# Keys, queries and values in token order: a change to how windowed attention gets its key tiles

## The chip, the cores and the metric

The kernel runs on one NeuronCore of a Trainium2 chip. The metric is the device time of one execution, in microseconds (us). A core has five engines, each with its own queue of instructions that it works off in order: PE (TensorE, the matrix unit; its weight loads are listed as PEld), DVE (VectorE), ACT (ScalarE), POOL (GpSimd) and SP (SyncE). DMA transfers are issued by SP and POOL here and run on 16 DMA engines beside them. A transfer that changes the type (a cast from float32 to bfloat16) is issued by POOL, a transfer that transposes by SP.

## What is computed

Attention over a window with eight global tokens, for 8 batches x 8 heads x 576 tokens x 64 dimensions, and then a two-layer network on the joined heads (4608 tokens, 512 -> 2048 -> 512), whose activation is h + sin(alpha h)^2 / alpha:

```python
scores = scale * np.matmul(q, k.transpose(0, 1, 3, 2))
mask = np.abs(pos[:, None] - pos[None, :]) <= 32
mask = mask | is_global[:, None] | is_global[None, :]
attn = softmax(np.where(mask, scores, -1e9))
x = (attn @ v).transpose(0, 2, 1, 3).reshape(B * S, H * D)
h = x @ w_in
s = np.sin(alpha * h)
out = (h + s * s / (alpha + 1e-09)) @ w_out
```

## The kernel before

**Stages.** The work is done batch by batch. `attention(b)` makes scores, weights, sums and the normalised x of batch b, transposed (`xT`). `gemm1(b)` multiplies by `w_in` in 16 groups of 128 columns (`nt`): PE makes a group of 8 matmuls in one of three PSUM tiles (`zn`, `zr`, `zd`), ACT takes the sine (L1192), ACT or DVE squares it (L1195, L1197), DVE adds and writes `H2` (L1198) and so frees the tile. `gemm2(b)` multiplies by `w_out`; its matmuls (L1250) are a generator, from which `fill` puts some between the other stages' matmuls on PE. The program is `phase_a(0)`, `gemm1(0)`, `phase_a(1)`, `gemm1(1)` and so on, where `phase_a(b)` is attention(b) with gemm2(b-1) mixed in. The instructions of an engine stand in the order of the program text.

**Key tiles.** The 576 keys of a batch are cut into 12 tiles of 48. A tile takes 64 columns of `KX`: its keys, the 8 global keys (`NG`), and zeros. Two heads lie on the 128 partitions. The rows of `VX` or `VF` (values) and of the mask have the same order as the columns of `KX`. Before, that order is: 24 even tokens, 8 global, 24 odd tokens, 8 empty. There are two `KX`, `QX` (queries, even and odd tokens apart) and value buffers, for even and odd batches.

**How batches 2 to 7 get their keys and queries.** `cast_qk(b)` (L334) casts keys and queries into DRAM (`kd`, `qd`) in large pieces, as they lie. `turn_qk(b)` (L350) transposes each in one DMA on SP into `kt` and `qt`. `place(b, which, t, y)` (L358) copies them on DVE into `KX` (L370) and `QX` (L363), in eight copies of 64 partitions x 1152 a batch: `which` is key or query, `t` the half of the tokens, `y` even or odd. `PLACES` lists the eight; `places_at` and the two tables `PLACED_SECOND` and `PLACED_LATE` say where they are done: for batch 2, two at the end of attention(1) and six in gemm1(1); for later batches, the four of keys in the attention stage before, at the third and fourth pair of heads, and the four of queries in the gemm1 that follows, at groups 5, 7, 9 and 11.

**Batches 0 and 1** get keys and queries another way (`load_lying`, `turn_lying`, `place_lying`: loaded with a cast by POOL, transposed on PE, copied from PSUM).

**Values.** For batches 2 to 7, `cast_v(b)` (L344) casts into DRAM by tokens and heads (`vd`, 4608 pieces of 64 elements), `load_v(b)` (L433) loads them in four DMAs and `load_vg(b)` (L437) adds the global rows. Batch 0 is loaded with a cast by POOL in twelve DMAs (`load_v0`, L396), tokens in pairs; DVE copies the odd rows to their place (`odd_rows`, L415) and four edge tiles are copied to `VE` (`edge_tile`, L419). Batch 1 is cast in pairs to `vpd` (L402), loaded in two DMAs (L408), and treated by `odd_rows` and `edge_tile` in the same way. In these two batches the global values are multiplied apart (`global_products`, L927, with weights `VGT`).

**What sets the order of the DMAs.** POOL issues casts and loads in one queue; `pace` (L348) is a small copy of some result, behind which POOL's next casts wait. SP issues transposes, loads, the stores of the output (L1283, from three tiles `osb`) and a store of logarithms for each pair of heads (L823, from five tiles). A DMA of either queue waits until the one eight before it has landed.

Of the kernel before, what the change touches and what calls it, by code (L numbers as in the profile page):

```python
# [29 lines left out]
PLACES = [(w, t, y) for w in (1, 0) for t in range(2) for y in range(2)]  # L30
# [220 lines left out]
def kernel(  # L251
# [47 lines left out]
    VF = [main.tile([P, NT6, H, 2, D], DT.bfloat16, name=f"VF{i}") for i in range(2)]  # L299
    VE = [main.tile([P, H, D], DT.bfloat16, name=f"VE{i}") for i in range(2)]  # L300
    vflat = [t[:].rearrange("p m h y d -> p (m h y d)") for t in VF]
# [12 lines left out]
    VGT = [main.tile([P, H, D], DT.bfloat16, name=f"VGT{i}") for i in range(2)]  # L314
    gkq = [main.tile([NG * B, NG, D], DT.bfloat16, name=f"gkq{i}") for i in range(2)]
    pick = main.tile([NG * B, 2, P], DT.bfloat16, name="pick")
# [14 lines left out]
    vpd = dramp.tile([HALF, H, 2, D], DT.bfloat16, name="vpd")  # L331

    def cast_qk(b):

        for src, name in ((k, "kd"), (q, "qd")):
            cast[b, name] = dramp.tile([P, H * S * D // P], DT.bfloat16, name=name)
            flat = (cast[b, name][:].rearrange("p f -> (p f)"), src[b].rearrange("h s d -> (h s d)"))
            dst, src_b = [t.rearrange("(a e c) -> e a c", a=16, e=16) for t in flat]
            nc.gpsimd.dma_start(out=dst, in_=src_b)

    def cast_v(b):

        cast[b, "vd"] = dramp.tile([S, H, D], DT.bfloat16, name="vd")
        nc.gpsimd.dma_start(out=cast[b, "vd"][:], in_=v[b].rearrange("h s d -> s h d"))  # L344
# [5 lines left out]
    def turn_qk(b):  # L350

        turned[b] = [trp.tile([P, H * HALF], DT.bfloat16, name=name) for name in ("qt", "kt")]
        for i in (1, 0):
            nc.sync.dma_start_transpose(
                out=turned[b][i][:], in_=cast[b, ("qd", "kd")[i]][:].rearrange("p (r c) -> (p r) c", c=P)
            )

    def place(b, which, t, y, copy, hps=slice(0, NHP)):  # L358

        src = turned[b][which][:].rearrange("p (hp t s) -> p t hp s", t=2, s=HALF)[y * D : (y + 1) * D, t, hps]  # L360
        rows = slice(t * D, (t + 1) * D)
        if which == 0:
            copy(  # L363
                out=QX[b % 2][rows, hps, y, PAD : PAD + 6 * SEG].rearrange("p h (m c) -> p h m c", c=SEG)[
                    :, :, :, 4:
                ],
                in_=src.rearrange("p h (m a) -> p h m a", a=KT),
            )
        else:
            copy(  # L370
                out=KX[b % 2][rows, hps, :, y * 32 : y * 32 + NH],
                in_=src.rearrange("p h (i a) -> p h i a", a=NH),
            )

    def place_globals(b, part, copy):

        if part == 0:
            copy(out=KX[b % 2][:, :, :, NH : NH + NG], in_=kTg[:, :, None, :, b].to_broadcast([P, NHP, NT12, NG]))
# [14 lines left out]
    def load_v0():  # L393
        for half in range(2):
            for m in range(NT6):
                nc.gpsimd.dma_start(  # L396
                    out=VF[0][half * D : half * D + NH, m].rearrange("p h y d -> p h (y d)"),
                    in_=v[0].rearrange("h (n m a y) d -> n m a h (y d)", n=2, a=NH, y=2)[half, m],
                )

    def cast_v1():
        nc.gpsimd.dma_start(  # L402
            out=vpd[:].rearrange("s h y d -> s h (y d)"), in_=v[1].rearrange("h (s y) d -> s h (y d)", y=2)
        )

    def load_v1():
        for half in range(2):
            nc.sync.dma_start(  # L408
                out=VF[1][half * D : half * D + NH].rearrange("p m h y d -> p m (h y d)"),
                in_=vpd[:].rearrange("(n m a) h y d -> n a m (h y d)", n=2, a=NH)[half],  # L410
            )

    def odd_rows(b, half, copy):
        r = half * D
        copy(out=VF[b][r + 32 : r + 32 + NH, :, :, 0], in_=VF[b][r : r + NH, :, :, 1])  # L415

    def edge_tile(b, half, y, copy):
        r, m, o = (1 - half) * D, half * (NT6 - 1), half * D + y * 32
        copy(out=VE[b][o : o + NH], in_=VF[b][r : r + NH, m, :, y])  # L419

    def edge_tiles(b, half, copy):
        for y in range(2):
            edge_tile(b, half, y, copy)

    def load_v(b):


        for half in range(2):
            m0 = half * (NT6 - 1)
            src = cast[b, "vd"][:].rearrange("(m a y) h d -> y a m (h d)", a=NH, y=2)[:, :, m0 : m0 + NT6 + 1]  # L430
            for y in range(2):
                r = half * D + y * 32
                nc.sync.dma_start(out=VX[b % 2][r : r + NH].rearrange("p m h d -> p m (h d)"), in_=src[y])  # L433

    def load_vg(b):
        for r in (NH, D + NH):
# [5 lines left out]
    def values(b, rows, half, i, h):  # L442

        if b > 1:
            return VX[b % 2][rows, i - half * (NT6 - 1), h, :]
        m = i - half * NT6
        return VF[b][rows, m, h, 0, :] if 0 <= m < NT6 else VE[b][rows, h, :]

# [58 lines left out]
    nc.gpsimd.iota(place8[:], pattern=[[0, 2], [NG, D]], base=-NG * NH, channel_multiplier=0,  # L507
# [18 lines left out]
    for t in (0, D):  # L526
        nc.sync.dma_start(out=gp64[t + NH : t + NH + NG], in_=global_idx[:, None])
        nc.sync.dma_start(
            out=gidx8[t + NH : t + NH + NG],
# [31 lines left out]
    for i, bits in enumerate((B - 1, D - 1, B * (NG - 1))):  # L561
# [6 lines left out]
    cond = setup.tile([P, 4], DT.float32, name="cond")  # L568
    odd, isg, off, iskey = [cond[:, i : i + 1] for i in range(4)]
    nc.vector.tensor_scalar(out=odd, in0=pm, scalar1=32.0, scalar2=None, op0=ALU.is_ge)  # L570
    nc.vector.scalar_tensor_tensor(out=isg, in0=pm, scalar=float(NH), in1=odd, op0=ALU.is_ge, op1=ALU.subtract)
    nc.vector.scalar_tensor_tensor(out=off, in0=pm, scalar=float(NK), in1=isg, op0=ALU.is_ge, op1=ALU.add)
    nc.vector.tensor_scalar(out=iskey, in0=off, scalar1=-1.0, scalar2=1.0, op0=ALU.mult, op1=ALU.add)
    nc.vector.tensor_scalar(out=kpos[:], in0=pm, scalar1=2.0, scalar2=None, op0=ALU.mult)
    nc.vector.scalar_tensor_tensor(out=kpos[:], in0=odd, scalar=-63.0, in1=kpos[:], op0=ALU.mult, op1=ALU.add)
    nc.vector.scalar_tensor_tensor(
        out=kpos[:], in0=off, scalar=float(4095 + KT), in1=kpos[:], op0=ALU.mult, op1=ALU.add
    )
# [864 lines left out]
```

## Time and profile before

| | us |
|---|---|
| median of 3 runs (lowest to highest) | 343.82 (343.78 to 345.46) |
| the profiled execution | 346.34 |
| its span, first to last instruction | 344.6 |
| mean granted PE clock | 0.995 |

The columns of the view of stages (windows) are: the stretch and its length, then busy time and count of instructions of PE, PEld, DVE, ACT and POOL, the granted clock of PE, the busy share of the DMA engines (over 1 where packets overlap) and the GB/s that they moved. A row of a group of instructions gives the line, engine and operation, the tiles written and read with their shape, the count, the busy time in us and the mean of one in ns, and the idle time before them. A row of the timeline gives start and duration in us; "[x <-y]" behind it is idle time ahead of it and what ended it. A row of the chain gives start, duration and what was done then on the path that ended last. SPq and POOL rows of DMAs are the time that it took to issue them.

### The profile page before, as it was taken

Reading aid. Unit: us, or ns where it says so; the run is one execution under the profiler, and the core shown is the slowest. Engines: PE = TensorE matmul, PEld = TensorE weight load, DVE = VectorE, ACT = ScalarE, POOL = GpSimd, SP = SyncE. Lnnn points to the kernel's source line nnn. Section 1 sums busy time; section 2 is a strip of 40 time slices with the busy share of each in tenths; the row PEclk is TensorE's granted clock in tenths of the full one; section 3 lists DMA queues with packets and bytes.
Section 4 is the critical chain, followed back from the end, with each engine's and each line's share of the span. In section 5 each row is a group of like instructions: output and inputs, shape, how many; then the busy total and the mean of one; then the engine's idle time right before and its main releaser. Section 6 shows DMA issues by size and latency. Waiting matters only on the chain.

```text
span 344.6 us, 11604 instructions
## 1 busy us (share of the span) xinstructions
PE 313.9 (91%) x4791; PEld 202.3 (59%) x4851; DVE 274.4 (80%) x535; ACT 282.8 (82%) x410; POOL 57.1 (17%) x90
## 2 busy tenths in 40 slices
PE   0778999999997999999999999999999999999993
PEld 0646765666554764677556655676566655665553
DVE  5886899789985698879886889789787988788930
ACT  9886988888997679988899789978898888889611
POOL 7982120120240000400040002200000000003600
PEclk9999999999998999999999999999999999999999
DMA  7999999999999546798449942993624111010232
GB/s 103 117 168 202 199 221 175 167 169 188 172 149 194 120 47 155 133 208 127 102 83 221 162 84 56 199 163 73 129 74 86 30 32 66 3 31 2 77 93 68
DMA packets 83021, 41.79 MB, mean 121 GB/s; under 512 B 65442, under 2 KB 74002, under 8 KB 82962
## 3 DMA queue, kind: packets, MB, share of 16 engines
q0 software_dynamic: 41600, 18.50, 43.3%
q1 hardware_dynamic: 41362, 22.48, 30.1%
q8 instruction: 39, 0.64, 0.8%
q14 instruction: 20, 0.16, 0.1%
HBM read 41.85 MB, written 20.77 MB: 182 GB/s over the span
## 4 chain that ended last, share of the span: by engine, by line
PE 66%; DMA 11%; DVE 7%; issue 5%; ACT 4%; POOL 4%; DVEq 0%; POOLq 0%; ACTq 0%
PE zo L1250 31%; PE zn L1150 10%; DMA w_out<-in_moe_w_out_dram 8%; PE zd L1150 7%; PE zr L1150 7%; DVE H L1198 5%; DMA w_in<-in_moe_w_in_dram 3%; PE ring L863 3%; PE zd L911 2%; PE zn L911 2%; POOL VF L396 2%; ACT sb L1192 2%; DVE s L1197 1%; DVE QX L363 1%; ACT s L1195 1%
## 5 line engine op out<-in xcount | busy, mean ns | idle before, releaser
L1250 PE MATMUL zo<-w_out,H 128*128 128x512 bf16 (+1 forms) x516 | 135.1, 378 | 6.3 <-issue 5.1
L1150 PEld LDWEIGHTS <-w_in 128*128 128x128 bf16 x1024 | 99.8, 98 | 50.0 <-issue 16.4
L1250 PEld LDWEIGHTS <-H 128*128 128x128 bf16 x592 | 54.0, 98 | 47.1 <-issue 1.3
L1150 PE MATMUL zn<-xT,w_in 128*128 128x288 bf16 (+1 forms) x384 | 57.0, 287 | 3.5 <-DVE H L1198 2.9
L1150 PE MATMUL zr<-xT,w_in 128*128 128x288 bf16 x320 | 47.9, 287 | 2.6 <-issue 2.0
L1192 ACT ACTIVATE sb<-zn,alphaT 128x576 bf16<-128x576 f32 (+1 forms) x48 | 35.6, 742 | 15.9 <-PE zn L1150 15.5
L1198 DVE SCALAR_TENSOR_TENSOR H<-s,recipT,zn 128x576 bf16<-128x576 bf16 (+1 forms) x48 | 39.5, 822 | 10.5 <-ACT s L1195 6.4
L1150 PE MATMUL zd<-xT,w_in 128*128 128x288 bf16 x320 | 47.1, 291 | 0.5 <-DVE H L1198 0.2
L871 ACT ACTIVATE E<-ring 128x720 bf16<-128x720 f32 x46 | 36.0, 782 | 9.4 <-PE ring L863 8.8
L1197 DVE TENSOR_TENSOR s<-sb 128x576 bf16<-128x576 bf16 (+1 forms) x70 | 32.6, 466 | 12.4 <-ACT sb L1192 12.1
L1195 ACT ACTIVATE s<-sb 128x576 bf16<-128x576 bf16 (+1 forms) x58 | 40.0, 689 | 1.8
L880 DVE TENSOR_TENSOR E<-E,MASKT 128x720 bf16<-128x720 bf16 x64 | 33.3, 528 | 5.6 <-ACT E L871 3.7
L1198 DVE SCALAR_TENSOR_TENSOR H<-s,recipT,zd 128x576 bf16<-128x576 bf16 (+1 forms) x40 | 32.9, 822 | 3.8 <-ACT s L1195 1.1
L1198 DVE SCALAR_TENSOR_TENSOR H<-s,recipT,zr 128x576 bf16<-128x576 bf16 (+1 forms) x40 | 32.9, 822 | 3.1 <-ACT s L1195 0.7
L1192 ACT ACTIVATE sb<-zd,alphaT 128x576 bf16<-128x576 f32 (+1 forms) x40 | 29.6, 739 | 5.9 <-PE zd L1150 5.9
L1192 ACT ACTIVATE sb<-zr,alphaT 128x576 bf16<-128x576 f32 (+1 forms) x40 | 29.6, 739 | 5.3 <-PE zr L1150 5.2
L1257 ACT COPY osb<-zo 128x512 f32<-128x512 f32 (+1 forms) x36 | 21.0, 583 | 10.7 <-PE zo L1250 7.0
L863 PEld LDWEIGHTS <-KX 64*64 64x64 bf16 x896 | 15.7, 113 | 19.6 <-issue 19.0
L828 ACT ACTIVATE R<-L,shift 128x576 f32<-128x576 f32 x32 | 25.0, 785 | 1.3 <-DVE xT L954 0.8
L1240 POOL COPY H<-H 128x11 bf16 (+1 forms) x16 | 7.2, 453 | 99.0 <-DVE H L1198 98.1
L348 POOL COPY seen<-xT 1x1 bf16<-1x1 bf16 x4 | 1.9, 479 | 106.7 <-DVE GN L805 106.7
L954 DVE TENSOR_TENSOR xT<-zn,R 128x576 bf16<-128x576 f32 x22 | 16.6, 753 | 2.9 <-ACT R L828 0.9
(181 smaller groups left out, 361.9 us busy)
## 6 DMA issues: line engine op xcount, KB each, us to landing
VF<-vd SPq DMA_DIRECT2D x24, 168.0 KB
kd<-in_k_dram POOLq DMA_DIRECT2D x6, 576.0 KB, 8.3
qd<-in_q_dram POOLq DMA_DIRECT2D x6, 576.0 KB, 16.1
vd<-in_v_dram POOLq DMA_DIRECT2D x6, 576.0 KB, 13.0
w_in<-in_moe_w_in_dram POOLq DMA_DIRECT2D x2, 1024.0 KB, 15.9
w_out<-in_moe_w_out_dram POOLq DMA_DIRECT2D x2, 1024.0 KB
out_dram<-osb SPq DMA_DIRECT2D x7, 256.0 KB
out_dram<-osb SPq DMA_DIRECT2D x8, 224.0 KB
```

The source lines that it names most:

```text
L828: nc.scalar.activation(out=R[:], in_=L[:], func=AF.Exp, scale=-1.0, bias=shift[:, 0:1])
L863: nc.tensor.matmul(out=z[half * D : (half + 1) * D, t, 0 : G3 * WCOL].rearrange("p (m x c) -> p m x c", x=2, c=60)[:, m % G3, :, c0:c1], l ...
L871: nc.scalar.activation(out=weights(hp, g), in_=z[:, :, 0 : G3 * WCOL], func=AF.Exp, scale=scale)
L880: nc.vector.tensor_tensor(out=Eg, in0=Eg, in1=MASKT[:, None, G3 * g : G3 * (g + 1), :].rearrange("p o m c -> p o (m c)").to_broadcast([P, ...
L954: nc.vector.tensor_tensor(out=xT[:, hp, 0:S].rearrange("p (k m c) -> p k m c", k=4, c=KT), in0=tokens(nd(hp, 0)), in1=Rs[hp][:], op=ALU.mult,)
L1150: nc.tensor.matmul(out=h_part, lhsT=w_in[:, c, nt * P : (nt + 1) * P], rhs=xT[:, c, lo:hi], start=(c == 0), stop=(c == CT - 1), skip_group ...
L1192: nc.scalar.activation(out=sb[:, 0:W], in_=h, func=AF.Sin, scale=alphaT[:, nt : nt + 1])
L1195: nc.scalar.activation(out=s2[:, 0:W], in_=sb[:, 0:W], func=AF.Square)
L1197: nc.vector.tensor_tensor(out=s2[:, 0:W], in0=sb[:, 0:W], in1=sb[:, 0:W], op=ALU.mult)
L1198: nc.vector.scalar_tensor_tensor(out=H2[:, nt, r0 : r0 + W], in0=s2[:, 0:W], scalar=recipT[:, nt : nt + 1], in1=h, op0=ALU.mult, op1=ALU.add,)
L1250: nc.tensor.matmul(out=ops[:, cols], lhsT=H2[:, nt, blk * P : (blk + 1) * P], rhs=w_out[:, nt, cols], start=(nt == 0), stop=(nt == NT - 1) ...
L1257: nc.scalar.copy(out=osb[:, cols], in_=ops[:, cols])
```

## The change

The order inside a key tile becomes token order: 48 keys, 8 global, 8 empty. With it:

* Keys of batches 2 to 7 are turned by 12 DMA transposes of 48 tokens each, straight into `KX`; `kt` and the copies of keys go. Queries are turned by 2 transposes (even and odd tokens) and placed by 2 copies on 128 partitions.
* Casts of keys and queries are by tokens, as those of values were.
* Values are loaded with one DMA for each half of the tiles, not two. Batch 1 is treated as the later ones (no `vpd`, `odd_rows`, `VE`, nor products with global values); batch 0 keeps its twelve loads, now with single tokens and 48 partitions, and has two edge copies inside `VX`.
* Places: the query copies for batch 2 stand at the end of attention(1), those for batch b+1 at the third pair of heads of attention(b). The casts for batch b+2 move from attention(b) to the second group of gemm1(b). The cast of v(1) and the loads of `w_out` stand with the other loads at the start, with no wait on the first batch ahead of them.

```diff
     def cast_qk(b):
-        for src, name in ((k, "kd"), (q, "qd")):
-            cast[b, name] = dramp.tile([P, H * S * D // P], DT.bfloat16, name=name)
...
-            dst, src_b = [t.rearrange("(a e c) -> e a c", a=16, e=16) for t in flat]
-            nc.gpsimd.dma_start(out=dst, in_=src_b)
+        cast_heads(b, k, "kd")
+        cast_heads(b, q, "qd")
+    def cast_heads(b, src, name):
+        cast[b, name] = dramp.tile([S, H, D], DT.bfloat16, name=name)
+        nc.gpsimd.dma_start(out=cast[b, name][:], in_=src[b].rearrange("h s d -> s h d"))
     def turn_qk(b):
-        turned[b] = [trp.tile([P, H * HALF], DT.bfloat16, name=name) for name in ("qt", "kt")]
-        for i in (1, 0):
+        kd, qd = [cast[b, name][:].rearrange("s h d -> s (h d)") for name in ("kd", "qd")]
+        for i in range(NT12):
+            nc.sync.dma_start_transpose(out=KX[b % 2][:, :, i, 0:KT], in_=kd[i * KT : (i + 1) * KT])
+        turned[b] = trp.tile([P, NHP, 2, HALF], DT.bfloat16, name="qt")
+        for y in range(2):
             nc.sync.dma_start_transpose(
-                out=turned[b][i][:], in_=cast[b, ("qd", "kd")[i]][:].rearrange("p (r c) -> (p r) c", c=P)
+                out=turned[b][:, :, y, :], in_=qd.rearrange("(s y) c -> y s c", y=2)[y]
             )
-    def place(b, which, t, y, copy, hps=slice(0, NHP)):
...
+    def place_queries(b, y):
+        nc.vector.tensor_copy(
+            out=QX[b % 2][:, :, y, PAD : PAD + 6 * SEG].rearrange("p h (m c) -> p h m c", c=SEG)[:, :, :, 4:],
+            in_=turned[b][:, :, y, :].rearrange("p h (m a) -> p h m a", a=KT),
+        )
     def load_v0():
-                    out=VF[0][half * D : half * D + NH, m].rearrange("p h y d -> p h (y d)"),
-                    in_=v[0].rearrange("h (n m a y) d -> n m a h (y d)", n=2, a=NH, y=2)[half, m],
+                    out=VX[0][half * D : half * D + KT, m + half],
+                    in_=v[0].rearrange("h (n m a) d -> n m a h d", n=2, a=KT)[half, m],
+    def edge_tile(half):
+        r, o = half * D, (1 - half) * D
+        m = (1 - half) * NT6
+        nc.vector.tensor_copy(out=VX[0][r : r + KT, m], in_=VX[0][o : o + KT, 1 if m else NT6 - 1])
-    clear(vflat[1].bitcast(DT.float32))
-    clear(VE[1][:].rearrange("p h d -> p (h d)").bitcast(DT.float32))
...
+    cast_v(1)
+    load_w_out((0, 1))
     gather_heads(k, gk)
...
         def numerators(hp):
             products(hp, 0)
-            if b < 2:
-                global_products(hp)
             normalise(hp)
...
-            if 0 < b < B - 1 and nt in late:
-                place(b + 1, *PLACES[late[nt]], nc.vector.tensor_copy)
...
-                load_v1()
+                load_v(1)
+                load_vg(1)
                 cast_qk(2)
-            if b == 0 and nt == NT - 2:
-                odd_rows(1, 0, nc.vector.tensor_copy)
+            if 1 < b and b + 2 < B and nt == CASTS:
+                pace(H2[0:1, 0, r0 : r0 + 1])
+                cast_qk(b + 2)
+                cast_v(b + 2)
...
-            for which, t, y in places_at(b_att, at):
-                place(b_att + 1, which, t, y, nc.vector.tensor_copy)
+            if b_att + 1 < B and at == (NHP if b_att == 1 else 2):
+                for y in range(2):
+                    place_queries(b_att + 1, y)
```

What this does to the order is shown at three places. First POOL, at the start of the program, behind the last load of keys and queries for batch 1. Before:

```order
L482 DMA H_99<-in_q_dram 48x4x768
L982 COPY seen<-VE_93 1x1
L402 DMA vpd<-in_v_dram 2304x1x128
L458 DMA w_out<-in_moe_w_out_dram 128x8x512 x2
L766 CAST gkq_109<-SQ 64x512
L766 CAST gkq_108<-SQ 64x512
L339 DMA kd<-in_k_dram 16x16x1152
L339 DMA qd<-in_q_dram 16x16x1152
```

Now:

```order
L449 DMA H_97<-in_q_dram 48x4x768
L333 DMA vd<-in_v_dram 4608x1x64
L425 DMA w_out<-in_moe_w_out_dram 128x8x512 x2
L717 CAST gkq_106<-SQ 64x512
L717 CAST gkq_105<-SQ 64x512
L333 DMA kd<-in_k_dram 4608x1x64
L333 DMA qd<-in_q_dram 4608x1x64
```

The copy that waited for the first batch's edge tiles is gone, the cast of v(1) has twice the pieces, and those of batch 2's keys and queries have 4608 where they had 256.

Second SP, from the logarithms of batch 0 to the first stores of the output, in attention(1). Before:

```order
L823 DMA LC<-L 2x576 x4
L408 DMA VF_92<-vpd 24x6x1024 x2
L354 DMA_TRANSPOSE kt<-kd 128x2304
L354 DMA_TRANSPOSE qt<-qd 128x2304
L823 DMA LC<-L 2x576
L1283 DMA out_dram<-osb 128x512
```

Now:

```order
L774 DMA LC<-L 2x576 x4
L400 DMA VF_92<-vd 48x7x512 x2
L407 DMA VF_92<-VGb 8x7x512 x2
L350 DMA_TRANSPOSE KX_93<-kd 128x4x48 x12
L353 DMA_TRANSPOSE qt<-qd 128x4x288 x2
L774 DMA LC<-L 2x576
L1225 DMA out_dram<-osb 128x512
```

Two transposes have become fourteen at the same place, and batch 1 gets its global values by two more loads.

Third DVE, in gemm1(2), groups 2 to 7. Before:

```order
L1198 SCALAR_TENSOR_TENSOR H_99<-s_2805,recipT,zn 128x576
L1197 TENSOR_TENSOR s_2820<-sb 128x576
L1198 SCALAR_TENSOR_TENSOR H_99<-s_2820,recipT,zr 128x576
L363 COPY QX_98<-qt 64x4x6x48
L1198 SCALAR_TENSOR_TENSOR H_99<-s_2835,recipT,zd 128x576
L1197 TENSOR_TENSOR s_2849<-sb 128x576
L1198 SCALAR_TENSOR_TENSOR H_99<-s_2849,recipT,zn 128x576
L363 COPY QX_98<-qt 64x4x6x48
L1198 SCALAR_TENSOR_TENSOR H_99<-s_2865,recipT,zr 128x576
```

Now:

```order
L1140 SCALAR_TENSOR_TENSOR H_97<-s_2761,recipT,zn 128x576
L1139 TENSOR_TENSOR s_2776<-sb 128x576
L1140 SCALAR_TENSOR_TENSOR H_97<-s_2776,recipT,zr 128x576
L1140 SCALAR_TENSOR_TENSOR H_97<-s_2790,recipT,zd 128x576
L1139 TENSOR_TENSOR s_2804<-sb 128x576
L1140 SCALAR_TENSOR_TENSOR H_97<-s_2804,recipT,zn 128x576
L1140 SCALAR_TENSOR_TENSOR H_97<-s_2819,recipT,zr 128x576
```

The query copies between the groups are gone; the two that remain stand in the attention stage before.

More of the change, by code (lines that the diff above doesn't have):

```diff
@@ L442, in values @@
     def values(b, rows, half, i, h):
[L444 to L447, printed above, removed]
+        return VX[b % 2][rows, i - half * (NT6 - 1), h, :]
     def load_w_in(gs):
@@ L1343, in beside @@
                 if at == 3:
[L1344 removed]
+                    lay_global_values()
                 return
[L1346 to L1349 removed]
             if b_att == 2 and at == 0:
@@ L1378 @@
         if b == 1:
-            pace(turned[2][0][0:1, 0:1])
+            pace(turned[2][0:1, 0, 0, 0:1])
             cast_v(2)
```

167 lines of the change are left out of this document (46 added, 121 removed).

## The prediction

> **What bounds the kernel now.** I read the page first: the table of busy time, then the chain of work that ended last.
>
> ```profile
> PE 313.9 (91%) x4791; PEld 202.3 (59%) x4851; DVE 274.4 (80%) x535; ACT 282.8 (82%) x410; POOL 57.1 (17%) x90
> PE 66%; DMA 11%; DVE 7%; issue 5%; ACT 4%; POOL 4%; DVEq 0%; POOLq 0%; ACTq 0%
> ```
>
> PE is the bound, but 34% of the chain is something else, so the question is in which stage. The ACT table loads mark the borders of the stages; the view of windows, cut there, gives busy times. The rows are: attention(1), gemm1(1), attention(2), gemm1(2), gemm1(3), gemm1(5).
>
> ```profile
> 51.09:68.12 17.03, 16.23 (x415) 9.43 (x420) 14.55 (x31) 14.49 (x23) 0.76 (x2) 1.00 1.03 177
> 68.12:89.58 21.46, 20.17 (x143) 13.93 (x143) 19.39 (x32) 18.45 (x27) 2.73 (x3) 1.00 1.12 172
> 89.58:105.56 15.98, 15.13 (x383) 8.86 (x388) 13.73 (x29) 14.52 (x23) 6.26 (x6) 1.00 1.29 167
> 105.56:130.04 24.48, 22.27 (x146) 14.85 (x147) 17.77 (x29) 18.18 (x26) 0.00 (x0) 0.93 0.83 108
> 146.02:166.65 20.63, 20.53 (x148) 14.42 (x148) 17.57 (x29) 17.51 (x26) 0.00 (x0) 1.00 1.12 172
> 219.62:240.62 21.00, 20.31 (x144) 14.06 (x145) 17.56 (x29) 17.99 (x27) 0.00 (x0) 1.00 0.90 130
> ```
>
> After length come PE, PEld, DVE, ACT, POOL, PE's clock, DMA share and GB/s. Attention takes 16.0 us a batch, but 17.03 in batch 1. gemm1 takes 20.6 to 21.5, with DVE at 17.6 to 19.4: close behind PE. Whether DVE sets the pace shows in the chain, asked for by stage; the next rows are for 68:90, 105.5:130, 183:204, 220:241 and 257:278.
>
> ```profile
> by line: DVE H L1198 26.5%; ACT sb L1192 13.6%; issue 11.9%; PE zn L1150 10.4%; ACT s L1195 9.4%; DVE s L1197 7.7%; PE zo L1250 5.9%; ACT L1037 5.8%; PE zr L1150 5.2%; DVE QX L363 3.3%; DVE KX L370 2.1%; ACT osb L1257 0.7%; DVEq L1198 0.4%
> by line: PE zd L1150 20.1%; PE zn L1150 19.8%; PE zo L1250 19.3%; PE zr L1150 17.2%; issue 12.1%; DVE H L1198 7.1%; DVE QX L363 3.7%; DVE s L1197 1.6%; DVEq L1198 0.1%
> by line: PE zd L1150 24.8%; PE zo L1250 23.1%; PE zn L1150 21.7%; PE zr L1150 19.1%; DVE H L1198 7.8%; DVE QX L363 2.2%; DVE s L1197 1.8%; issue 1.5%; DVEq L1198 0.1%
> by line: PE zn L1150 21.4%; PE zd L1150 14.7%; PE zr L1150 14.6%; PE zo L1250 13.3%; DVE H L1198 12.2%; ACT L1037 6.1%; issue 5.4%; DVE QX L363 4.3%; DVE s L1197 4.0%; ACT sb L1192 3.1%; ACT osb L1257 2.8%; DVEq L1198 0.2%; ACTq L1192 0.0%
> by line: PE zn L1150 19.2%; DVE H L1198 16.2%; PE zo L1250 13.3%; PE zd L1150 10.0%; PE zr L1150 9.7%; issue 9.3%; ACT sb L1192 6.7%; DVE s L1197 5.8%; DVE QX L363 4.3%; ACT s L1195 3.3%; ACT osb L1257 2.7%; DVEq L1198 0.3%; ACTq L1192 0.1%
> ```
>
> So the copies that the change removes (L363, L370) stand on the path in five of the six gemm1 stages; in gemm1(3), where PE is busy 20.53 of 20.63, they do not.
>
> **The base.** The profiled execution took 346.34 us (span 344.6, and 1.74 around it), 2.5 above the median of 343.82. One stage breaks the pattern, gemm1(2) with 24.48 us. There PE stops, and then runs at half clock:
>
> ```profile
> 106.00:107.00 1.00, 0.01 (x1) 0.00 (x0) 0.46 (x2) 0.99 (x2) 0.00 (x0) 1.00 1.08 207
> 110.00:111.00 1.00, 1.00 (x5) 0.61 (x4) 0.90 (x2) 0.97 (x3) 0.00 (x0) 0.50 2.44 156
> ```
>
> The stage is 3.5 to 3.9 us over its neighbours. I take that as an event of this one execution, make the sum against the trace, and put its result on the median.
>
> **Gain 1: DVE copies.** Before, each of batches 2 to 7 has four copies of queries, which this row of the groups by line sums up, and as many of keys (L370), three of them in 1.43 us below:
>
> ```profile
> L363 DVE COPY QX<-qt 64x1152 bf16<-64x1152 bf16 x24 | 10.9, 453 | 0.6
> ```
>
> After, two a batch remain, on twice the partitions and as many elements in each, so 453 ns each: 48 copies become 12, 16.5 us of DVE. What counts is what stood on the path, and the gemm1 stages now hold no copy at all, but for the two at the start of gemm1(1). The shares times the windows: gemm1(1) 5.4% of 22 = 1.19, gemm1(2) 3.7% of 24.5 = 0.91, gemm1(4) 2.2% of 21 = 0.46, gemm1(5) and (6) 4.3% of 21 = 0.90 each: **4.4 us**. The pace agrees. In gemm1(4), before and after the copies begin:
>
> ```profile
> 190.35 0.98 PE zn L1150 x8
> 191.55 0.98 PE zr L1150 x8
> ...
> 197.79 1.12 PE zn L1150 x8
> 199.12 1.07 PE zr L1150 x8
> ```
>
> A group takes 1.20 us and then 1.33; 0.13 over seven groups is 0.9 us a stage, 5.5 for six. Bounds: nothing (PE or ACT sets the pace anyway) to 5.5. In attention I count nothing: its PE is the same in batches with and without these copies.
>
> **Gain 2: attention(1).** Its 32 products with global values (L927) go, and its odd rows and edge tiles. Attention(2), which has none, is 17.03 - 15.98 = **1.05 us** shorter. Bounds 0.5 to 1.05.
>
> **Costs 1: the start, which is DMA.** The chain over the whole execution has two transfers, and PE's timeline the matmuls that follow the second:
>
> ```profile
> 16.45 11.95 DMA w_in<-in_moe_w_in_dram
> 28.68 26.91 DMA w_out<-in_moe_w_out_dram
> ...
> 55.64 2.10 PE L1250 MATMUL zo<-w_out,H 128*128 128x512 bf16 x8
> ```
>
> The first w_in half lands at 28.40, where gemm1(0) begins; the second w_out half lands at 55.59, and PE's first matmuls with it are at 55.64. Both are just in time. From 19 to 57 us the DMA engines are never idle, so whatever is made longer ahead of w_out in POOL's queue delays PE by as much. Three things are:
>
> ```profile
> 9.03 7.44 POOL L396 DMA_DIRECT2D VF<-in_v_dram  x12
> 23.92 1.33 POOL L402 DMA_DIRECT2D vpd<-in_v_dram  x1
> 67.54 2.20 POOL L344 DMA_DIRECT2D vd<-in_v_dram  x1
> 30.00:33.00 3.00, 1.97 (x17) 1.46 (x15) 1.54 (x3) 2.39 (x4) 0.60 (x1) 1.00 1.15 208
> 223.00:224.00 1.00, 0.55 (x5) 0.31 (x4) 1.00 (x2) 1.00 (x2) 0.00 (x0) 1.00 2.46 157
> ```
>
> (a) Twelve value loads, 0.62 us to issue each, with 192 pieces, now have 384. 2304 pieces (vpd) cost 1.33 us and 4608 (vd) 2.20, so 0.38 ns a piece: 12 x 192 x 0.38 = 0.87 us, until w_in is issued. (b) The cast of v(1) takes 4608 pieces in place of 2304. Casts in big pieces move 208 GB/s (30 to 33 us), in small ones 157 (223 to 224 us): 0.59 MB in 2.84 or in 3.75 us, at most 0.9 more; vpd lies between, I take 0.65. (c) Values of batch 1 now arrive as 0.80 MB with their global rows, not 0.59: 1.0 us at 208 GB/s, not all of it ahead of w_out, so 0.8. The sum is **2.3 us** when PE reaches the second w_out half. Issuing w_out earlier gains nothing, for the queue is full. Bounds: 0 to 4.
>
> What the first batch saves (odd rows and edge tiles on DVE, two clears on ACT) and gemm1(0) (odd rows of batch 1) counts nothing: the same two landings are late next. Were they not, it would be worth some 1 us, the 0.95 of that copy on DVE.
>
> **Costs 2: queries of batch 2.** SP waits for kd, turns it, then qd. The rows are from the timeline, and at the end from the view of a tile and from the page's DMA issues:
>
> ```profile
> 58.44 3.33 SPq L354 DMA_TRANSPOSE kt<-kd  x1
> 61.87 3.39 SPq L354 DMA_TRANSPOSE qt<-qd  x1
> 67.30 0.18 POOL L348 COPY seen<-qt 1x1 bf16<-1x1 bf16 x1 [18.52 <-DMA qt<-qd]
> 68.94 1.65 DVE L370 COPY KX<-kt 64x1152 bf16<-64x1152 bf16 x2
> 86.17 3.08 SPq L354 DMA_TRANSPOSE kt<-kd  x1
> 99.74 1.43 DVE L370 COPY KX<-kt 64x1152 bf16<-64x1152 bf16 x3
> 238.12 2.35 SPq L354 DMA_TRANSPOSE kt<-kd  x1
> 251.22 1.38 DVE L370 COPY KX<-kt 64x1152 bf16<-64x1152 bf16 x3
> L433 SPq DMA_DIRECT2D VF<-vd x24: 291/384/535, 77.2 to 258.1; - x24
> vd<-in_v_dram POOLq DMA_DIRECT2D x6, 576.0 KB, 13.0
> ```
>
> On an idle queue a whole transpose is issued in 2.35 us (238.12). A twelfth of its rows is 0.2, and a small DMA's fixed part about 0.3 (the least of L433): I take 0.5 us for a key tile, 1.2 for half the queries. Bounds: 0.3 (the L433 row) and 3.3 (a whole transpose's row) each. kd lands at 58.44 + 2.3 + 0.9 = 61.6; twelve tiles end at 67.6, queries at 70.0, and land 2.0 later (as 67.30 stands to 61.87 + 3.39): 72.0. DVE meets the copies at 68.94 + 2.3 - 1.05 = 70.2, waits 1.8, and has gemm1's first squares behind them, 1.0 us late: **1.0 us**. Bounds 0 to 4.
>
> In later batches the queries are due at the third pair of heads, where three key copies stand now, 13 us after SP starts to turn (86.17 to 99.74, 238.12 to 251.22; batch 4 likewise). 12 x 0.5 + 2 x 1.2 + 2.0 = 10.4 us: covered, by about 2.5. Output stores and sums behind them on SP go out 3 us later than now; three output tiles take that up: nothing. Casts are issued at the second group of gemm1 and turned at its end, some 17 us later; vd, the like of them, lands after 13.0: nothing. POOL issues 4.5 us more a batch; a pair of DVE copies beside a cast (67.54) took 1.65 us in place of 0.9, three beside another (99.74) their usual 1.43. So 0 to 0.7 us a cast; a gemm1 stage leaves DVE 3 us of 20.6, and I take nothing.
>
> The Trainium skill (DMA: Bandwidth & Descriptors, Specifications) asks for 512 B a piece at least for the full rate; these casts write 128. The rows above agree in kind (157 against 208 GB/s), and the price is taken from them.
>
> **Sum:** -4.4 - 1.05 + 2.3 + 1.0 = -2.1 us; 343.82 - 2.1 = **341.7 us**.
>
> **Rivals.**
> 1. *Transposes too slow* (slower). If a key tile costs 0.85 us and half the queries 1.6, turning takes 15.4 us with the landing; DVE, and PE behind it, waits about 5 us in batch 2 and 2 in each of the three tight ones. 341.7 + 4 + 6 = 352. It decides from about 0.7 us a tile. For it: six whole transposes took 1.9 to 6.1 us, so SP can be held up. Against: the idle-queue row. The Trainium skill (same page, Rules for kernel authors) says that transfers under 64 KB are mostly overhead; a tile is 48 KB. Chance 0.18.
> 2. *DMA at the start has slack* (faster): no costs, 343.82 - 5.4 = 338.4. For it: the earlier issue of w_out and v(1). Against: a queue without a gap. Chance 0.17.
> 3. *PE or ACT keeps gemm1's pace* and only the costs and attention(1) count: 343.82 + 2.25 = 346.1. For it: gemm1(3); ACT is at 17.5 to 18.5 in these stages. Chance 0.12.
> 4. *A PE pause as at 106 us comes in more executions*, since casts crowd into gemm1: 341.7 + 3.6 = 345.3. The Trainium skill (TensorE: Matmul & The Clock Gate, Part 1) has the clock halve after an idle window of about 3.4 us; here 2 us were enough. Chance 0.08.
>
> The forecast has the remaining 0.45.
>
> **How the numbers follow.** A measurement tells 0.5% (1.7 us) from no change, so faster is below 342.1 and slower above 345.5. The forecast's own range is 339.5 to 344, two thirds of it faster. Faster: 0.30 + 0.17 = 0.47. Same: 0.15 + 0.08 + 0.05 = 0.28. Slower: 0.18 + 0.07 = 0.25. The range 336.5 to 352 leaves out the slow half of rival 1 and the extremes.
>
> **What would show it.** Right: no L363 or L370 kind of copy in gemm1, spacing near 1.20 us there to the end of the stage, attention(1) near 16.0; w_out landing near 58; the first query copy at about 72; key tiles 0.5 us apart on SP. Wrong: DVE waiting for qt in attention(2), (3) or (6) (rival 1); w_in and w_out landing no later than now (rival 2); gemm1 no shorter without copies (rival 3); a stage with clock under 1.00 (rival 4).

## The result: slower by 15%, and the profile after

| | before | after |
|---|---|---|
| median of the runs on one chip | 344.64 us (343.78 to 346.4) | 396.47 us (395.4 to 397.28) |
| span of the profiled execution | 344.6 us | 394.5 us |
| mean granted clock of TensorE | 0.995 | 0.928 |

The ratio is 1.149, 95% interval 1.1435 to 1.1554. The predicted 341.7 us and the range up to 352 are both missed; so is every rival's time. First the page of after, its busy times and its chain:

```profile
PE 321.3 (81%) x4759; PEld 208.2 (53%) x4818; DVE 258.8 (66%) x483; ACT 279.0 (71%) x407; POOL 75.1 (19%) x89
PE 61%; SPq 11%; DVE 9%; DMA 7%; ACT 5%; issue 4%; POOL 1%; DVEq 0%; POOLq 0%; ACTq 0%
```

DVE does 16 us less work than before, as forecast, and the execution is 50 us longer: the time went into waiting. SPq, the queue of SyncE, has 11% of the chain; in the chain of before it had no entry at all. The windows cut at the ACT table loads tell where. In this order: gemm1(1), attention(2), (3) and (6), gemm1(5) and (6), with the columns of the prediction's first table.

```profile
68.94:106.80 37.86, 21.05 (x141) 14.37 (x142) 21.61 (x26) 18.58 (x28) 7.07 (x4) 0.77 1.09 124
106.80:130.56 23.76, 15.53 (x377) 9.34 (x381) 12.71 (x27) 14.51 (x23) 2.37 (x2) 0.83 0.82 96
152.72:177.77 25.05, 15.52 (x377) 9.35 (x382) 12.72 (x31) 14.84 (x23) 0.00 (x0) 0.85 0.31 78
281.86:306.51 24.65, 15.94 (x379) 9.53 (x383) 12.54 (x27) 14.85 (x23) 0.00 (x0) 0.87 0.35 82
260.26:281.86 21.60, 21.50 (x149) 15.05 (x150) 15.61 (x25) 18.00 (x27) 6.80 (x4) 0.95 1.57 145
306.51:327.78 21.27, 21.17 (x152) 14.89 (x152) 15.73 (x25) 17.41 (x25) 0.00 (x0) 0.99 0.26 51
```

Before, attention(3) and (6) were:

```profile
130.04:146.02 15.98, 15.13 (x382) 8.72 (x387) 13.64 (x32) 14.84 (x24) 3.87 (x4) 1.00 0.70 150
240.62:257.05 16.43, 15.57 (x384) 8.91 (x389) 13.17 (x29) 14.86 (x24) 0.00 (x0) 1.00 0.51 109
```

gemm1(1) is 16.4 us longer than before, attention(2), (3) and (6) are 7.8, 9.1 and 8.2 longer, with PE just as busy in attention as it was: PE stands still there. The next rows are from the view of waits (waiting engine and line, releaser; total, times, longest) and from the view of the two lines of transposes (least, median and longest duration in ns, first and last start).

```profile
DVE QX L359 <- DMA qt<-qd: 46.0, 12, 10.3
PE zn L862 <- DVE GN L756: 29.1, 5, 8.5
L350 SPq DMA_TRANSPOSE KX<-kd x72: 1177/1235/2693, 59.3 to 295.5; - x72
L353 SPq DMA_TRANSPOSE qt<-qd x12: 1280/1328/2004, 76.7 to 298.2; - x12
```

DVE waits 46.0 us for turned queries, and in the five attention stages PE waits 29.1 for what is queued behind that on DVE. A key tile costs SP **1.235 us** (the median), where I had put 0.5; half the queries, with six times the data, cost 1.33. So the transpose of a key tile has nearly all of the price of one six times its size. Batch 3 in the timelines of SP and DVE and in the chain:

```profile
103.59 16.75 SPq L350 DMA_TRANSPOSE KX<-kd  x12
120.51 3.33 SPq L353 DMA_TRANSPOSE qt<-qd  x2
124.77 0.46 DVE L359 COPY QX<-qt 128x1152 bf16<-128x1152 bf16 x1 [7.72 <-DMA qt<-qd]
...
125.89 0.04 DVE QX L359
125.92 0.34 issue
126.26 0.53 DVE E L831
126.79 0.67 DVE xT L908
127.46 0.14 DVE GN L756
127.60 0.04 issue
127.64 0.79 PE zn L862 x25
```

SP issues these transposes from 103.59 to 123.8, 20 us and not 8.4; the masks and normalisations that PE needs stand behind the waiting copy in DVE's order. PE's clock then falls (windows of half a microsecond; PE ended its last matmul at 120.43):

```profile
122.00:122.50 0.50, 0.00 (x0) 0.00 (x0) 0.00 (x0) 0.00 (x0) 0.00 (x0) 1.00 2.01 198
122.50:123.00 0.50, 0.00 (x0) 0.00 (x0) 0.00 (x0) 0.00 (x0) 0.00 (x0) 0.58 1.84 40
...
132.50:133.00 0.50, 0.50 (x4) 0.39 (x3) 0.00 (x0) 0.00 (x0) 0.00 (x0) 0.68 0.00 0
```

The granted clock is halved 2.2 us after PE stopped, and stays halved until 5 us after it has work again. The Trainium skill (TensorE: Matmul & The Clock Gate, Part 1) puts the idle window at about 3.4 us. Here the clock fell 2.2 us into an idle stretch; at 106 us before, it fell after a pause of 1.96 us, when PE was at work again.

One stall had no place in my sum. The timelines of DVE and of POOL at gemm1(1):

```profile
80.13 0.46 DVE L359 COPY QX<-qt 128x1152 bf16<-128x1152 bf16 x1 [10.29 <-DMA qt<-qd]
81.39 6.12 DVE L359 COPY QX<-qt 128x1152 bf16<-128x1152 bf16 x1 [0.80 <-DMA qt<-qd]
...
80.59 2.19 POOL L333 DMA_DIRECT2D vd<-in_v_dram  x1
82.27 2.74 POOL L333 DMA_DIRECT2D kd<-in_k_dram  x1
83.96 3.27 POOL L333 DMA_DIRECT2D qd<-in_q_dram  x1
```

Two equal copies: the first takes 0.46 us, the second 6.12, and it ends (87.51) 0.3 us after POOL has issued the last of three casts (87.23, which is 83.96 + 3.27).

### The profile page after: what moved, and what is told of

It is laid out like the page before. It is cut to its first block, busy times and chain, and to the rows that moved or that the text cites. A ratio compares the mean times of both kernels' runs of the same rounds, so it can differ in the third digit from the quotient of the medians.

```text
span 394.5 us, 11569 instructions
## 1 busy us (share of the span) xinstructions
PE 321.3 (81%) x4759; PEld 208.2 (53%) x4818; DVE 258.8 (66%) x483; ACT 279.0 (71%) x407; POOL 75.1 (19%) x89
## 3 DMA queue, kind: packets, MB, share of 16 engines
HBM read 41.95 MB, written 20.77 MB: 159 GB/s over the span
## 4 chain that ended last, share of the span: by engine, by line
PE 61%; SPq 11%; DVE 9%; DMA 7%; ACT 5%; issue 4%; POOL 1%; DVEq 0%; POOLq 0%; ACTq 0%
PE zo L1192 22%; PE zn L1092 12%; SPq L350 10%; PE zr L1092 9%; PE zd L1092 8%; DMA qt<-qd 6%; DVE H L1140 3%; PE zd L862 2%; PE ring L814 2%; DVE QX L359 2%; PE zn L862 1%; SPq L353 1%; ACT sb L1134 1%; DVE xT L908 1%; DMA H<-in_q_dram 1%
## 5 line engine op out<-in xcount | busy, mean ns | idle before, releaser
L1192 PE MATMUL zo<-w_out,H 128*128 128x512 bf16 (+1 forms) x517 | 136.8, 381 | 6.6 <-issue 5.9
L1092 PEld LDWEIGHTS <-w_in 128*128 128x128 bf16 x1024 | 102.7, 101 | 64.3 <-issue 27.3
L1092 PE MATMUL zn<-xT,w_in 128*128 128x288 bf16 (+1 forms) x384 | 61.1, 301 | 18.7 <-DVE H L1140 18.0
L1092 PE MATMUL zr<-xT,w_in 128*128 128x288 bf16 x320 | 49.8, 296 | 0.3 <-DVE H L1140 0.2
L1092 PE MATMUL zd<-xT,w_in 128*128 128x288 bf16 x320 | 46.3, 288 | 0.4 <-DVE H L1140 0.2
L359 DVE COPY QX<-qt 128x1152 bf16<-128x1152 bf16 x12 | 11.2, 932 | 46.0 <-DMA qt<-qd 46.0
L862 PE MATMUL zn<-E,VF 56*64 56x120 bf16 (+2 forms) x616 | 11.6, 216 | 29.1 <-DVE GN L756 29.1
L862 PEld LDWEIGHTS <-VF 56*64 56x64 bf16 x896 | 16.5, 122 | 35.1 <-issue 33.4
L344 POOL COPY seen<-H 1x1 bf16<-1x1 bf16 x5 | 0.9, 178 | 153.8 <-DVE H L1140 153.8
## 6 DMA issues: line engine op xcount, KB each, us to landing
w_out<-in_moe_w_out_dram POOLq DMA_DIRECT2D x2, 1024.0 KB, 28.6
```

What stands on the lines that cost most here:

```text
L862: nc.tensor.matmul(out=nd(hp, key)[t * D : (t + 1) * D, half, :, a - half * CUT : z - half * CUT], lhsT=ones[rows, 0:D] if key else values ...
L1092: nc.tensor.matmul(out=h_part, lhsT=w_in[:, c, nt * P : (nt + 1) * P], rhs=xT[:, c, lo:hi], start=(c == 0), stop=(c == CT - 1), skip_group ...
L1192: nc.tensor.matmul(out=ops[:, cols], lhsT=H2[:, nt, blk * P : (blk + 1) * P], rhs=w_out[:, nt, cols], start=(nt == 0), stop=(nt == NT - 1) ...
```

## The experiments

**Is it the number of transposes, and do they harm by delay or by holding SP?** Theory A is the price per instruction. The first kernel (keys_whole) turns the keys once, into a staging tile:

```diff
-        for i in range(NT12):
-            nc.sync.dma_start_transpose(out=KX[b % 2][:, :, i, 0:KT], in_=kd[i * KT : (i + 1) * KT])
+        keys_of[b] = trp.tile([P, NHP, S], DT.bfloat16, name="kt")
+        nc.sync.dma_start_transpose(out=keys_of[b][:], in_=kd)
...
+                for y in range(2):
+                    place_keys(b_att + 1, y)
                 for y in range(2):
                     place_queries(b_att + 1, y)
```

> The twelve key transposes of a batch become one of all 576 tokens into a staging tile, and two DVE copies of 0.46 us put it into the key tile; casts, queries and all else as in the change. Theory A (a transpose has a price per instruction of some 1.2 us on SP's queue, nearly independent of its size, and DVE waits for queries that stand behind twelve of them): keys are turned in about 2.4 us in place of 15 to 17, DVE's wait for qt (46.0 us in the change) falls below 3 us, attention(2) to (6) take 16 to 17 us each, the clock is back near 1.00, and the time is 348 to 354 us; what remains over 344.6 is mostly the copy of 6.12 us. Theory B (the time goes by the bytes or the 128 B pieces of kd that a transpose reads): turning the keys still takes 12 us or more, the wait stays, and the time stays above 385 us.

Measured: 346.91 us (346.28 to 349.0), ratio to before 1.0072, interval 1.003 to 1.0114. Its windows are 15.96 to 16.40 us in attention(2) to (6), and the wait for qt is gone. Its gemm1(1) and attention(2):

```profile
69.24:95.46 26.22, 21.12 (x142) 14.49 (x142) 21.02 (x28) 18.57 (x27) 5.51 (x3) 0.93 1.45 142
95.46:111.42 15.96, 15.11 (x383) 8.84 (x388) 13.33 (x29) 14.50 (x22) 2.37 (x2) 1.00 1.04 128
```

Theory A holds: of the 52 us lost, 49.6 go with eleven of the twelve transposes. By the spans of the stages, after against this kernel, that is 30.6 us in attention(2) to (6), 11.6 in gemm1(1), and 7.4 in gemm1(2) to (6), stages in which nothing waits for queries. The clock was 0.94 to 0.99 in these five; the share of it that was missing, times their lengths, gives an estimate of 4.9 us of the 7.4. In the change they also hold all 128 of their matmuls with `w_in`; in this kernel two to four of the 128 lie outside the borders.

The second kernel (queries_first) has all fourteen transposes, those of queries first:

```diff
+        turned[b] = trp.tile([P, NHP, 2, HALF], DT.bfloat16, name="qt")
+        for y in range(2):
+            nc.sync.dma_start_transpose(
+                out=turned[b][:, :, y, :], in_=qd.rearrange("(s y) c -> y s c", y=2)[y]
+            )
         for i in range(NT12):
             nc.sync.dma_start_transpose(out=KX[b % 2][:, :, i, 0:KT], in_=kd[i * KT : (i + 1) * KT])
```

> The same fourteen transposes as in the change, but the two of queries are issued ahead of the twelve of keys. Theory A with the queue's order as the whole harm: the queries land some 5 us after turning begins, DVE no longer waits in attention(2) to (6), the twelve key transposes still take 14 to 18 us on SP, and the time is 346 to 353 us, within 4 us of keys_whole. Rival A2 (SP held for 15 us also makes the output stores and the sums late, and ACT or PE waits for their tiles): DVE's wait goes as well, but ACT waits for output tiles, and the time is 355 to 370 us.

Measured: 362.33 us, ratio 1.0516 (1.0485 to 1.0547), 15 us above keys_whole: rival A2 holds. The wait for queries is gone, and a new one has come, here in gemm1(5), from its waits, SP's timeline and its window:

```profile
ACT osb L1199 <- DMA out_dram<-osb: 7.6, 1, 7.6
...
227.02 8.03 SPq L355 DMA_TRANSPOSE KX<-kd  x5
235.15 0.99 SPq L1225 DMA_DIRECT2D out_dram<-osb  x2
...
228.93:259.20 30.27, 22.06 (x144) 14.95 (x145) 15.69 (x25) 18.02 (x27) 6.79 (x4) 0.83 1.30 140
```

The output stores stand behind the transposes on SP, ACT has no free output tile until one has gone, PE waits for what follows in ACT's order, and the clock falls: 30.27 us for a stage of 21.00 before. I had written that three output tiles take up a delay of 3 us; they do not take up one of 15.

**What the price goes by.** Six transposes of 96 tokens (keys_six), and four of one pair of heads each (keys_by_pair), both into the staging tile:

```diff
+        for i in range(6):
+            rows = slice(i * 2 * KT, (i + 1) * 2 * KT)
+            nc.sync.dma_start_transpose(out=keys_of[b][:, :, rows], in_=kd[rows])
...
+        for hp in range(NHP):
+            nc.sync.dma_start_transpose(out=keys_of[b][:, hp], in_=kd[:, hp * P : (hp + 1) * P])
```

> As keys_whole, but the keys of a batch are turned by six transposes of 96 tokens into the staging tile: the dose between twelve (396.5 us) and one (346.9 us). Theory A (1.2 to 1.3 us an instruction): the keys take about 7.5 us, with 2.7 for the queries and 2.0 to land some 12 us, just inside the 13 us after which DVE wants the queries: attention(3) to (6) wait at most about 1 us each and the time is 346 to 350 us. If the price goes by tokens, six take as long as one (about 2.5 us on an idle queue) and the time is that of keys_whole within 0.5 us; if harm grows evenly with the number of transposes, it is about 369 us (346.9 + 5 of 11 parts of 49.6).

> As keys_whole, but by four transposes, each of all 576 tokens and of one pair of heads (one run of 1152 B on each partition; a key tile of the change has four runs of 96 B). Price by instruction: 1.2 to 1.4 us each on an idle queue, about 5 us in all. Price by run: about 0.31 us each (a quarter of 1.24), 1.2 us in all. Price by bytes: a quarter of the whole transpose's 2.6 us each, 0.65. The time stays within 2 us of keys_whole in each case, so the durations decide.

The lines of these transposes in the first and in the second kernel:

```profile
L352 SPq DMA_TRANSPOSE kt<-kd x36: 1219/1257/2095, 59.8 to 254.7; - x36
...
L351 SPq DMA_TRANSPOSE kt<-kd x24: 1169/1263/2570, 60.1 to 246.3; - x24
```

48 KiB cost 1.235 us, 96 KiB 1.257, 144 KiB in runs of 1152 B 1.263, 288 KiB 1.328: up to there the price is by instruction, neither by byte nor by run. A whole transpose of keys (576 KiB) took 2.60 us at least in keys_whole, and 2.35 before, so above 288 KiB the size counts; where that begins, no run shows.

The time of the six was 355.41 us (ratio 1.0334, 1.028 to 1.0387), outside what I expected (346 to 350) and below the even line (369). Attention(3) to (6) took the 16.0 to 16.4 us of keys_whole, so there six are covered. Nearly the whole loss is in gemm1(1), 31.64 us against 26.22, where DVE waits 3.1 us for both turned tiles and a copy again takes 6.15, and in attention(2), 19.59 against 15.96, where the two query transposes took 5.08 us and not 2.7. So the harm doesn't grow evenly: it begins where a batch's slack ends, and batches 2 and 3, turned in attention(1) and gemm1(1), have the least. The four took 348.93 us in one run, with 28.52 us in gemm1(1) and 16.66 in attention(2).

**The copy of 6 us.** In the change, POOL's casts start when the first half of the queries has landed, so beside the second copy. Here (pace_behind) they start behind it:

```diff
-            pace(turned[2][0:1, 0, 0, 0:1])
+            pace(QX[0][0:1, 0, 1, PAD + 4 : PAD + 5])
```

> As the change, but in gemm1(1) POOL's casts wait until both query copies are in the query tile, not for the landed queries. Theory P (the second copy took 6.12 us in place of 0.46 because POOL was issuing casts from 80.6 to 87.2 us beside it): both copies take 0.46 us, gemm1(1) is 5 to 6 us shorter, and the time is 389 to 392.5 us. Rival (the copy was long for another cause, its source or the transposes in flight): it stays at about 6 us and the time at 395 to 398 us.

Measured: 389.66 us, ratio 1.1322 against 1.1494, so 6.8 us less. DVE and POOL in this kernel:

```profile
80.97 0.46 DVE L359 COPY QX<-qt 128x1152 bf16<-128x1152 bf16 x1 [0.70 <-DMA qt<-qd]
81.35 0.45 DVE L1139 TENSOR_TENSOR s<-sb 128x576 bf16<-128x576 bf16 x1
81.91 0.81 DVE L1140 SCALAR_TENSOR_TENSOR H<-s,recipT,zn 128x576 bf16<-128x576 bf16 x1
...
81.93 2.19 POOL L333 DMA_DIRECT2D vd<-in_v_dram  x1
```

Theory P holds, and the operations of two inputs beside the same issues keep their usual 0.45 and 0.81 us. To see whether it is the copy's form, keys_whole with its copies written as a maximum (placed_by_max; the queries' copies likewise):

```diff
-        nc.vector.tensor_copy(
-            out=KX[b % 2][:, hps, :, 0:KT], in_=keys_of[b][:, hps].rearrange("p h (i a) -> p h i a", a=KT)
-        )
+        src = keys_of[b][:, hps].rearrange("p h (i a) -> p h i a", a=KT)
+        nc.vector.tensor_tensor(out=KX[b % 2][:, hps, :, 0:KT], in0=src, in1=src, op=ALU.max)
```

> As keys_whole, with its order and its early casts, but the four copies of a batch are written as the maximum of the tile with itself, an operation of two inputs, which took 0.45 to 0.81 us per 576 columns beside POOL's issues in the change, when a copy of the same time stood still. If it is the copy's form that POOL's issues hold up: none of the four takes more than 0.9 us at 70 us, gemm1(1) is 3.5 to 4.5 us shorter than in keys_whole (26.2), and the time is 342 to 344.5 us. If any write of DVE beside these casts is held, or any with that source: one of the four takes about 5 us and the time stays at 347 us.

Measured: 344.05 us (342.68 to 344.81), ratio 0.9983 (0.9959 to 1.0006), so 2.9 us under keys_whole. DVE and POOL in keys_whole, then in this kernel:

```profile
70.06 5.33 DVE L362 COPY KX<-kt 128x1152 bf16<-128x1152 bf16 x2
...
68.12 2.19 POOL L333 DMA_DIRECT2D vd<-in_v_dram  x1 [0.26 <-issue]
```

```profile
71.09 1.42 DVE L363 TENSOR_TENSOR KX<-kt 128x1152 bf16<-128x1152 bf16 x2
72.42 1.42 DVE L368 TENSOR_TENSOR QX<-qt 128x1152 bf16<-128x1152 bf16 x2
...
68.94 2.19 POOL L333 DMA_DIRECT2D vd<-in_v_dram  x1 [0.26 <-issue]
```

The same work at the same place beside the same issues: 5.33 us for two copies, 1.42 for two maxima. Of the two copies the first took 4.97 us, until 75.03, and POOL's last issue ended at 74.75; the second took its usual 0.45. gemm1(1) falls from 26.22 to 21.40. A maximum takes 0.75 us undisturbed and a copy 0.45, and attention(3) to (6) are 0.4 to 0.6 us longer each for it.

The Trainium skill (SBUF — State Buffer, Who interferes with whom) says that DVE and GpSimd share a pair of ports by an exclusive lock, that a copy can run in a mode that takes both ports, that `tensor_tensor` takes only the read side of the pair, and that issue order decides who blocks; that descriptor generation needs the write side it calls inferred. The runs fit this, the direction included: the copy was held and the maximum was not, and POOL's issues came first and DVE lost. The ports and the lock themselves no run here shows.

**Are the gains there?** First a kernel (all_whole) meant to be without both stalls, with the queries turned by one transpose:

> keys_whole and pace_behind together, and the queries by one transpose (288 rows of two tokens) in place of two: two transposes a batch, four DVE copies on 128 partitions in place of eight on 64 in the kernel before. If my sum's gains are right (4.4 us in gemm1, less four copies that now stand in attention, and 1.05 in attention(1)) and its costs at the start (2.3 us), with the two events of the change removed: 340 to 344 us, faster than before by about 1 us. If PE or ACT keeps gemm1's pace (my rival 3): 345 to 348 us.

Its edit is that of keys_whole and of pace_behind, and

```diff
+            out=turned[b][:].rearrange("p y h s -> p (y h) s"), in_=qd.rearrange("(s y) c -> s (y c)", y=2)
```

Measured: 346.75 us, ratio 1.0072 (1.0054 to 1.0091), which by the expectation speaks for rival 3; but the windows say otherwise. gemm1(3) to (6) are 20.33 to 20.44 us, all shorter than before, and 4.8 us are lost in attention(2) alone. The casts start at 72.7 us here and not at 68, the two transposes of batch 3 take 7.75 and 5.38 us while the DMA engines work off other transfers, and DVE waits 5.3 us for qt. So this run doesn't weigh the gains. The next two do: keys_whole with early casts, batch 2 copied when POOL's issues are over (placed_later), and the same with the edge tiles of batch 0 on ACT.

```diff
+            if b == 1 and nt == 9:
+                place_batch(2)
             if 1 < b and b + 2 < B and nt == CASTS:
...
-        nc.vector.tensor_copy(out=VX[0][r : r + KT, m], in_=VX[0][o : o + KT, 1 if m else NT6 - 1])
+        nc.scalar.copy(out=VX[0][r : r + KT, m], in_=VX[0][o : o + KT, 1 if m else NT6 - 1])
```

> As keys_whole, but the four copies of batch 2 stand in the middle of gemm1(1), at its tenth group, when POOL has issued its three casts, and the casts start as early as in keys_whole. If POOL's issues are what held one copy for 4.9 us: all four take 0.46 us, gemm1(1) is 4 to 5 us shorter than in keys_whole (26.2), attention(2) keeps its 16.0, and the time is 341 to 343 us. If the stall moves to other work of DVE: it stays at 345 to 347.

> placed_later, and the two edge tile copies of batch 0 on ACT in place of DVE. On DVE the pair took 2.88 us in the change, beside POOL's issue of the cast of v(1) and of w_out, and 0.67 where that issue came after them (pace_behind, whose attention(1) began at 49.63 us, not 51.6 to 53.7 as in the others). If the stall of the pair is what makes the start of the change late: attention(1) begins at 49.5 to 51 us and the time is 339 to 341.5 us, 1.5 to 2.5 us under placed_later, and faster than the kernel before by about 1%. If w_out's landing holds the start (my prediction): no change against placed_later.

Measured: 341.54 us, ratio 0.9911 (0.9881 to 0.9941), and 340.89 us, ratio 0.9881 (0.9839 to 0.9922). **Both beat the kernel before**, by 0.9% and 1.2%: small, but both intervals lie below 1. Against each other the intervals leave them equal. The windows of the second, for attention(1), gemm1(1), (2) and (3):

```profile
51.23:67.71 16.48, 15.21 (x383) 8.80 (x387) 11.80 (x25) 14.63 (x23) 0.00 (x0) 1.00 1.85 175
67.71:89.00 21.29, 19.36 (x142) 13.83 (x142) 16.39 (x28) 18.58 (x28) 6.82 (x4) 1.00 1.67 165
106.45:127.22 20.77, 20.24 (x147) 14.34 (x147) 16.08 (x25) 17.90 (x26) 6.81 (x4) 1.00 1.67 153
143.19:163.61 20.42, 20.32 (x148) 14.45 (x148) 15.80 (x25) 17.52 (x25) 6.81 (x4) 1.00 1.64 147
```

The clock is 1.00 in these stages. For the start, the rows are: the edge copies of the change, in the timeline and in the chain, those of pace_behind, where they began before POOL's issue of the cast of v(1) at 21.76, and PE's second half of w_out in the kernel with these copies on ACT.

```profile
22.12 2.88 DVE L393 COPY VF<-VF 48x512 bf16<-48x512 bf16 x2
...
22.12 2.33 DVE VF L393
24.48 0.53 DVE VF L393
...
21.24 0.67 DVE L393 COPY VF<-VF 48x512 bf16<-48x512 bf16 x2
...
55.74 2.10 PE L1210 MATMUL zo<-w_out,H 128*128 128x512 bf16 x8 [0.69 <-DMA w_out<-in_moe_w_out_dram]
```

The pair of edge copies is held beside POOL's issue like the other copies, 2.88 us against 0.67. With them on ACT, attention(1) began 1.1 us earlier than in placed_later (51.23 against 52.34), and PE waited 0.69 us for w_out, which landed at 55.7. Attention(1) still ended 1.9 us earlier; 1.5 of that went in attention(2) (17.45 against 15.97 us), where DVE waited 1.30 us for the second half of the queries. Both profiled executions have a span of 339.8 us. So w_out, which I had expected to hold the start, took 0.69 us here, and the queries of batch 3 more. The kernel with pace_behind, whose attention(1) began earliest, at 49.63, waited 1.9 us for w_out.

**A second profile of the kernel before**, for the pause at 106 us:

> The kernel before, once more, for a second profile: if the pause of PE at 106 us, which made gemm1(2) 24.48 us, was an event of the one execution, gemm1(2) is 20.6 to 21.5 us here and the span 341 to 342 us; if it belongs to the kernel, gemm1(2) is again about 24.5 us.

gemm1(2) took 22.58 us there (one run, 348.24 us), with PE idle for 1.6 us at 110 to 111.6 and the clock at 1.00 throughout. So it is neither of the two: the pause comes again, behind the same matmul (the second into `zr`), but shorter. In the kernels above in which DVE waits at most 1.3 us for queries in attention(2), gemm1(2) takes 20.77 to 20.78. What makes the pause is open; it wasn't tried.

## Why the prediction was wrong, point by point

- **Costs 2, the price of a key tile, is the step that failed.** It put 0.5 us: a twelfth of a whole transpose by rows, and a plain DMA's fixed part. Measured, 1.235 us, and 1.257 for twice the rows: almost nothing goes by rows. The value was inside the bounds (0.3 to 3.3), but I took one near the low end, and the range was built on 0.85 at most. Two things ought to have stopped me: the bounds were a factor of ten apart, and twelve times any value above 0.7 broke the cover that I had worked out myself. Queries of batch 2 were 8 us later than forecast at DVE (first copy at 80.13 and not 72), and DVE waited 11.1 us, not 1.8.
- **Rival 1 had the mechanism** (DVE, and PE behind it, waits for queries turned late; decides from about 0.7 us a tile) and too small a size: 352. As measured, twelve tiles took 16.5 to 18.5 us of SP's time a batch, 20 to 22 with the queries and the landing, 7 to 9 over the 13 us of slack: the waits were 8.4, 9.7, 4.0, 4.0 and 8.9 us in attention(2) to (6). Two things came on top that it did not count: the halved clock (some 4.9 us in gemm1(2) to (6) alone, by the estimate above), and the held copy in gemm1(1). Rival 4's sign, stages with a clock under 1.00, came too, but behind these waits.
- **"Output stores go out 3 us later: nothing"** holds for a few us more than I had put: in keys_six, where the keys hold SP for 7.8 to 9.0 us, ACT waits for no store. It fails for 15: queries_first is 15 us slower than keys_whole, and ACT waits 14.8 us for stores there. In the change itself ACT waits for none.
- **"0 to 0.7 us a cast, I take nothing"** for POOL's issues was wrong by 5.7 us. The row with the pair of copies at 1.65 us beside a cast was the sign; I set it against three undisturbed copies at 99.74 as if the casts were alike. The copies at 68.94 stood beside a cast of 4608 pieces (2.20 us of issue at 67.54); those at 99.74 stood beside the casts of keys and queries, then of 256 pieces (0.61 and 0.56 us of issue from 99.72). The change makes these 4608 pieces too, 2.74 and 3.27 us of issue. In the second profile of the kernel before, the pair stood behind POOL's issues, at 72.59, and took its usual 0.91 us. Three such casts back to back make one closed stretch of 6.6 us, and in five of the kernels a copy that fell into it lasted until about its end.
- **Gain 1 (4.4 us)** is there, but partly capped by PE. In the last kernel (placed_later with the edge tiles on ACT) against before: gemm1(4) 0.62 us (forecast 0.46), (5) 0.59 (0.90), (6) 0.36 (0.90), (3) 0.21 (nothing), and (1), taken from all_whole, where its copies stand ahead of its groups, 0.99 (1.19). PE is then busy 20.32 of 20.42 us: rival 3 decides how much of the copies' time comes back. gemm1(2) gave 3.7 us against a forecast of 0.91, for the pause is not in it there.
- **Gain 2 (1.05 us)**: attention(1) is 16.2 to 16.5 us in most of these kernels against 17.03, so 0.5 to 0.8.
- **Costs 1 (2.3 us by w_out's landing)** was near in size by chance (1.7 us in the profiled execution) and wrong in cause. The second half of w_out was issued at 26.83 us, earlier than before (28.68), and took 28.6 to land, 55.4, no later than before (55.59), so that w_out had the slack of rival 2. Attention(1) began late in the change, at 52.75 and not 51.09, and the chain of its start runs through the two held edge copies. That they are the cause is likely, not shown, for one execution says little here: the start of attention(1) came out between 49.6 and 54.0 us in kernels whose start is the same, and at 55.02 in the second profile of before.

The direction of the gains was right, and 340.9 us was to be had from them in another arrangement; the way in which the keys reached their tile cost 49.6 us.

## What to carry to other kernels

Count DMA transposes before their bytes (up to 288 KiB each, here), and treat a doubtful price by where it would break the schedule: if the cover holds up to 0.7 us and the bounds go to 3.3, the forecast hangs on one number that has no row, and the range must say so. A wait on an in-order engine costs whatever stands behind it there, and a queue that is held costs everything that is issued after it, so look for both when a step is moved. Keep plain copies on DVE out of the stretches in which POOL issues casts of thousands of small pieces, or give them another form.

## What the runs showed of the hardware that was not expected

- A DMA transpose held SP for 1.24 to 1.33 us from 48 to 288 KiB, as medians; whole ones, at 576 KiB, took from 1.9 us (queries in the kernel before) to 7.75 beside other transfers (keys in all_whole).
- A DVE copy beside POOL's issues of three casts of 4608 pieces took 5.0 to 6.4 us in place of 0.46, in five kernels; maxima (0.75 us), products (0.45) and reductions (0.22) beside such issues took their usual durations.
- TensorE's granted clock fell to 0.50 some 2.2 us after PE's last matmul in attention(2) of the change, and came back 5 us after PE had work again.
